# The products with v and with kv in two column halves of the TensorE array

## The chip, the cores and the metric

The kernel runs on one core of a Trainium2 chip. The metric is the device time of one execution in microseconds (us), lower is better; each number of a comparison is the median of several executions. Engines are named as the profile names them: PE is TensorE's matmul, PEld its weight load, DVE is VectorE, ACT is ScalarE, POOL is GpSimd, SP issues the transfers.

## The reference

Three stages follow each other: an attention with random features, a layer of experts of which each token takes one, and a gated feed-forward layer. The change lies in the first alone, so the other two are cut.

```python
# q, k, v: 4 batches, 8 heads, 576 tokens, 64 numbers; omega: 128 features x 64
def phi(x):
    proj = np.einsum('bhsd,md->bhsm', x, omega)
    h = proj - np.sum(x * x, axis=-1, keepdims=True) / 2.0
    h = h - np.max(h, axis=-1, keepdims=True)
    return np.exp(h) / np.sqrt(m)
q_p, k_p = (phi(q * scale), phi(k * scale))
kv = np.einsum('bhsm,bhsd->bhmd', k_p, v)
z = np.sum(k_p, axis=2)
num = np.einsum('bhsm,bhmd->bhsd', q_p, kv)
den = np.einsum('bhsm,bhm->bhs', q_p, z)[..., None] + 1e-06
attn = num / den
...  # then the experts (2304 tokens, 512 wide, 8 experts) and the gated layer
```

## The kernel before, in words

The 2304 tokens (4 batches of 576) are 18 tiles of 128 tokens. Since 576 is four tiles and a half, the fifth of each nine tiles holds 64 tokens of one batch and 64 of the next; the code calls its index within the nine `MID`. The attention goes in two groups of two batches, each with nine k tiles and then nine q tiles, so 36 units, one per step of the loop `for s in range(N + 3)` (L577). Inside `tc.manual_schedule()` (L566) the order in which the code writes the instructions is the order in which each engine gets them. One step works on several units at different depths.

A step of a k tile: `project` (L403, matmul at L409) multiplies the tile with omega, two heads at a time, one in rows 0 to 63 and one in rows 64 to 127 of the array; DVE reduces to row maxima (`maxima`, L419) and ACT takes the exponentials (`exps`, L435) into `ph`, 128 tokens by 8 heads by 128 features. One step later `kv_sum` calls `kv_part` (L440, matmul at L448): for each head the stationary operand is `ph` of that head (128 tokens by 128 features) and the moving operand is 96 columns of v (64 of this head, a one for the sum z, and 31 that nobody reads). The results add up over the tiles of a batch in PSUM. For the `MID` tile `kv_part` runs twice, with 64 rows each time.

A step of a q tile: after `project`, `maxima` and `exps` as above, `turn` (L478, L482) transposes `ph` on TensorE, `turned` (L484, L496) copies the result to SBUF as `qt` (half by DVE, half by ACT), `numerators` (L499, L505) multiplies `qt` of each head (128 features by 128 tokens, stationary) with 96 columns of the batch's kv, `divide` (L511) is DVE's, and `turn_x` (L531, L534) transposes the quotient on TensorE. On TensorE a step therefore reads `project` of unit s, `turn_x` of s-3, `numerators` of s-2 and `turn` of s-1, with the router's products (L218, L230) between some. For the `MID` tile the transposed features are copied into two buffers, `qa` and `qb`, whose other 64 columns POOL set to zero early on (L627, L628), and each head takes two products, one with the first batch's kv and one with the second's, that add up in PSUM.

The operands here are float32. In the trace such a matmul is two load-and-product pairs (16 pairs for eight heads); a transpose is one.

Of the kernel before, what the change touches and what calls it, by code (L numbers as in the profile page):

```python
# [10 lines left out]
F32 = mybir.dt.float32  # L11
# [16 lines left out]
def attention_moe_ffn_kernel(  # L28
# [4 lines left out]
    nc = tc.nc  # L33
    NTI, _, DM2 = qx.shape
    DM = DM2 // 2
    D, M = om.shape[0] // 2, om.shape[1] // 2
    H = DM // D
    VW = D + 1
# [8 lines left out]
    PT = NTI // NP  # L47
    MID = PT // 2
# [14 lines left out]
    def bank(*shape):  # L63
        return psum.tile([128, *shape], F32, tag="one", name="one")
# [4 lines left out]
    def third():  # L69
        return psum.tile([128, 2, 512], F32, tag="third", name="third", bufs=1)  # L70
# [41 lines left out]
    wk = p1.enter_context(tc.tile_pool(name="wk", bufs=2))  # L112
# [245 lines left out]
    units = [(kind, g * PT + i) for g in range(NP) for kind in "kq" for i in range(PT)]  # L358
# [5 lines left out]

    with p1:
        HALF = (slice(0, DM // 2), slice(DM // 2, DM))
        loads, st, kv, acc = {}, [{} for _ in units], {}, {}

        def load(s):
            kind, i = units[s]  # L370
            t = ld.tile([128, 2, DM], F32, tag="kq", name=f"{kind}{i}", bufs=4)
            src = (kx if kind == "k" else qx)[i].rearrange("p (a d) -> p a d", a=2)
            if s == 0:
                for part in ((0, HALF[0]), (0, HALF[1]), (1, slice(None))):
                    nc.sync.dma_start(out=t[:, part[0], part[1]], in_=src[:, part[0], part[1]])
            else:
                nc.sync.dma_start(out=t, in_=src)
            loads[s] = t

        def load_v(s):  # L380
            i = tile_of(s, "k")
            if i is not None:
                t = loads["v", i] = ld.tile([128, VR], F32, tag="v", name=f"v{i}", bufs=4)
                nc.sync.dma_start(out=t, in_=vx[i])

        def squares(s):
            xn = loads[s][:, 1].rearrange("p (h d) -> p h d", d=D)
            sq = wk.tile([128, H, D], F32, tag="sq", name="sq", bufs=3)
            nc.gpsimd.tensor_tensor(out=sq, in0=xn, in1=xn, op=ALU.mult)
            kind, i = units[s]  # L390
            w = D
            while w > (D // 4 if kind == "q" and i % PT > 1 else D):
                w //= 2
                nc.gpsimd.tensor_tensor(
                    out=sq[:, :, 0:w], in0=sq[:, :, 0:w], in1=sq[:, :, w:2 * w], op=ALU.add
                )
            st[s]["sq"] = sq[:, :, 0:w]
# [42 lines left out]
        def kv_part(s, bt, rows, first, last):  # L440
            ph, vt = st[s]["ph"], loads["v", units[s][1]]
            if first and bt % 2:
                a = third()
                acc[bt] = [a[:, j, 0:384] for j in range(2)]
            elif first:
                acc[bt] = [bank(384) for j in range(2)]
            for h in range(H):
                nc.tensor.matmul(  # L448
                    acc[bt][h // 4][:, h % 4 * 96:(h % 4 + 1) * 96],
                    ph[rows, h, :], vt[rows, h * VW:h * VW + 96],  # L450
                    start=(first and h % 4 == 0), stop=last, skip_group_check=True,
                )

        def kv_sum(s):
            g, i = divmod(units[s][1], PT)
# [26 lines left out]
                nc.tensor.transpose(st[s]["t"][h // 4][:, h % 4, :], ph[:, h, :], ident)  # L482

        def turned(s):  # L484

            g, i = divmod(units[s][1], PT)
            if i == MID:
                parts = [(qa, 2 * g, slice(0, 64)), (qb, 2 * g + 1, slice(64, 128))]
            else:
                qt = wk.tile([128, H, 128], F32, tag="qt", name="qt")  # L490
                parts = [(qt, 2 * g + int(i > MID), slice(0, 128))]
            for hf in range(2):
                for qt, _, cols in parts:
                    src = st[s]["t"][hf][:, :, cols]
                    dst = qt[:, 4 * hf:4 * hf + 4, cols]
                    (nc.scalar.copy if hf else nc.vector.tensor_copy)(dst, src)  # L496
            st[s]["q"] = parts

        def numerators(s):  # L499
            a = third()  # L500
            st[s]["a"] = a[:, :, 0:384].rearrange("p a (h w) -> p a h w", w=96)
            parts = st[s]["q"]
            for h in range(H):
                for n, (qt, bt, _) in enumerate(parts):
                    nc.tensor.matmul(  # L505
                        st[s]["a"][:, h // 4, h % 4, :], qt[:, h, :], kv[bt][:, h * VW:h * VW + 96],
                        start=(n == 0 and h % 4 == 0), stop=(n == len(parts) - 1),
                        skip_group_check=True,
                    )

        def divide(s):  # L511
# [41 lines left out]
        load(3)  # L553
        load_v(2)
        om_s = wk.tile([128, 2 * M], F32, name="om_s", bufs=1)
        qa = wk.tile([128, H, 128], F32, name="qa", bufs=1)
        qb = wk.tile([128, H, 128], F32, name="qb", bufs=1)

        route = [Routing(0)]
        first = None  # L560
# [5 lines left out]
        with tc.manual_schedule():  # L566
            p = third()
            for _ in range(13):
                nc.tensor.matmul(p[:, 0, 0:128], ones, ones, start=True, stop=True)
            nc.vector.tensor_scalar(  # L570
                out=om_s, in0=om_raw, scalar1=SCALE, scalar2=None, op0=ALU.mult
            )
            squares(0)
            squares(1)
            router = router_stationary(emb_t)
            rest = route[0].rest()
            for s in range(N + 3):  # L577
                clock[0] = s
                if s + 4 < N:
                    load(s + 4)  # L580
                load_v(s + 3)
                if tile_of(s - 2, "k") is not None:
                    kv_out(s - 2)
                if tile_of(s - 2, "q") is not None:
                    turned(s - 2)
                if s + 2 < N:
                    squares(s + 2)
                old = tile_of(s - 3, "q")
                if old is not None:
                    token_norms(s - 3)  # L590
                if s < N:
                    project(s)
                t = tile_of(s - 6, "q")
                if t is not None and t % 3 == 2:
                    route[-1].logits(t % PT // 3)
                base = s - (2 * PT + 2)
                if base >= 1:
                    next(rest, None)
                if base == PT + 4:
                    route.append(Routing(1))  # L600
                if old is not None:
                    turn_x(s - 3)
                t = tile_of(s - 4, "q")
                group = t is not None and t % 3 == 2
                if group:
                    route[-1].products(t % PT // 3)
                if s > 1:
                    next(router, None)
                if s < N:
                    norms(s)  # L610
                    maxima(s)
                    exps(s)
                if old is not None:
                    turned_x(s - 3)
                if group:
                    route[-1].products_out()
                if s == PT + 4:
                    next(router, None)
                if tile_of(s - 2, "q") is not None:
                    numerators(s - 2)  # L620
                    divide(s - 2)
                if tile_of(s - 1, "k") is not None:
                    kv_sum(s - 1)
                if tile_of(s - 1, "q") is not None:
                    turn(s - 1)
                if s == 2:
                    nc.gpsimd.memset(qa[:, :, 64:], 0.0)  # L627
                    nc.gpsimd.memset(qb[:, :, 0:64], 0.0)  # L628
                if s == N:
                    first = Expert(0)  # L630
                if N <= s < N + 2:
                    first.fetch(nc.gpsimd)
# [14 lines left out]
    with ExitStack() as p2:  # L647
# [111 lines left out]
        last = xs[LAST]  # L759
# [3 lines left out]
        with tc.If(totals[0] > 0):  # L763
            for bt in range(B):
                with tc.For_i(0, E) as e:
                    n = nc.values_load(
                        ext_i[0:1, bass.ds(e + bt * E, 1)], min_val=0, max_val=S,
                        skip_runtime_bounds_check_because=why,
                    )
# [64 lines left out]
    with ExitStack() as p3:  # L834
# [25 lines left out]
        for grp in range(NF // GF):  # L860
            wos, h2s = [], [[] for _ in blocks]
            for ff in range(GF):
                f = grp * GF + ff
                w = wgv.pop(f) if f in wgv else gate_val(f)
                for nb, (t0, n) in enumerate(blocks):
                    cols = slice(t0 * 128, (t0 + n) * 128)
                    ps = pair()[:, :, 0:n * 128]
                    for m in range(2):
                        k = 0
                        for c in range(NC):  # L870
                            for a, x in HALVES:
                                nc.tensor.matmul(  # L872
                                    ps[:, m], w[:, a, m, c, :], xp[:, c, x, cols],
                                    start=(k == 0), stop=(k == 3 * NC - 1),
                                )
                                k += 1
                    s = sp.tile([128, 512], F32, tag="s", name="s")[:, 0:n * 128]
                    nc.scalar.activation(out=s, in_=ps[:, 0], func=AF.Silu)  # L878
                    nc.vector.tensor_tensor(out=s, in0=ps[:, 1], in1=s, op=ALU.mult)  # L879
                    h = h2p.tile([128, 2, 512], F32R, tag="h2", name="h2")[:, :, 0:n * 128]  # L880
# [78 lines left out]
```

## Time and profile before

| | us |
|---|---|
| time, median of 3 runs | 833.69 (833.52 to 835.24) |
| time of the profiled execution | 835.67 |
| its span, first to last instruction | 833.9 |
| PE busy in the span | 815.9 (98%) |
| weight loads (PEld) busy | 731.2 (88%) |
| DVE, ACT, POOL busy | 534.2, 273.5, 166.6 |

Read it with care: matmuls are pipelined and the record of one is far longer than the time until the next can start, so a busy share of 98% does not say that the array is used to the full. The distance between the starts of two loads, one after the other, is the better measure. The attention takes the first 175 us or so; the rest of the span is the experts and the gated layer, which the change does not touch.

### The profile page before, as it was taken

Reading aid. Unit: us, or ns where it says so; the run is one execution under the profiler, and the core shown is the slowest. Engines: PE = TensorE matmul, PEld = TensorE weight load, DVE = VectorE, ACT = ScalarE, POOL = GpSimd, SP = SyncE. Lnnn points to the kernel's source line nnn. Section 1 sums busy time; section 2 is a strip of 40 time slices with the busy share of each in tenths; the row PEclk is TensorE's granted clock in tenths of the full one; section 3 lists DMA queues with packets and bytes.
Section 4 is the critical chain, followed back from the end, with each engine's and each line's share of the span. In section 5 each row is a group of like instructions: output and inputs, shape, how many; then the busy total and the mean of one; then the engine's idle time right before and its main releaser. Section 6 shows DMA issues by size and latency. Waiting matters only on the chain.

```text
span 833.9 us, 12850 instructions
## 1 busy us (share of the span) xinstructions
PE 815.9 (98%) x5158; PEld 731.2 (88%) x5159; DVE 534.2 (64%) x919; ACT 273.5 (33%) x630; POOL 166.6 (20%) x165
## 2 busy tenths in 40 slices
PE   8989998999999998999999999999999999999998
PEld 7979997899999998999888888888888888888886
DVE  3797788776342342489994039837963993697354
ACT  3577657743131322432323332212211221122120
POOL 4352144030000000802222111211111121112120
PEclk8999999999999999999999999999999999999999
DMA  7644563132322222332211002200210120020014
GB/s 254 199 133 134 152 193 104 51 96 99 91 81 98 90 76 44 127 101 76 77 51 50 1 1 76 76 1 26 76 51 0 54 74 26 25 77 26 1 49 178
DMA packets 23676, 66.64 MB, mean 80 GB/s; under 512 B 3104, under 2 KB 5680, under 8 KB 23608
## 3 DMA queue, kind: packets, MB, share of 16 engines
q1 hardware_dynamic: 23608, 65.74, 24.9%
q8 instruction: 42, 0.69, 0.3%
q14 instruction: 26, 0.21, 0.1%
HBM read 60.94 MB, written 4.79 MB: 79 GB/s over the span
## 4 chain that ended last, share of the span: by engine, by line
PE 60%; DVE 0%; issue 0%
PE two L872 24%; PE one L845 18%; PE third L872 12%; PE two L678 3%; PE third L698 2%; PE two L698 2%; PE third L678 1%; DVE y_acc L854 0%
## 5 line engine op out<-in xcount | busy, mean ns | idle before, releaser
L872 PE MATMUL two<-xp,wp 128*128 128x512 f32 (+1 forms) x960 | 209.5, 368 | 0.0
L872 PEld LDWEIGHTS two<-xp,wp 128*128 128x128 f32 x960 | 168.2, 188 | 31.4 <-DVE s L879 0.6
L845 PE MATMUL one<-wo,h 128*128 128x512 f32 x648 | 159.8, 390 | 0.0
L90 POOL TENSOR_TENSOR h<-s,h 128x512 fp32r<-128x512 f32 (+1 forms) x60 | 78.1, 1303 | 337.8 <-ACT h L89 337.8
L845 PEld LDWEIGHTS one<-wo,h 128*128 128x128 f32 x648 | 120.6, 188 | 24.8 <-DVE y_acc L854 0.3
L854 DVE TENSOR_TENSOR y_acc<-y_acc,one 128x512 f32<-128x512 f32 x90 | 61.5, 684 | 77.3 <-PE one L845 77.2
L872 PE MATMUL third<-xp,wp 128*128 128x512 f32 (+1 forms) x480 | 106.5, 368 | 0.0
L872 PEld LDWEIGHTS third<-xp,wp 128*128 128x128 f32 x480 | 84.4, 188 | 15.4
L435 ACT ACTIVATE ph<-two,bias 128x128 f32<-128x128 f32 x288 | 78.1, 384 | 39.5 <-DVE bias L426 28.9
L678 PE MATMUL two<-xp,wp 128*128 128x288 f32 x576 | 82.4, 302 | 3.8 <-DVEq L763 3.8
L678 PEld LDWEIGHTS two<-xp,wp 128*128 128x128 f32 x576 | 79.9, 194 | 4.1 <-ACT xp L89 4.0
L89 ACT CAST h<-s 128x512 fp32r<-128x512 f32 (+1 forms) x60 | 34.7, 579 | 77.6 <-DVE s L879 77.6
L89 ACT CAST wp<-raw 128x1024 fp32r<-128x1024 f32 x32 | 33.6, 1049 | 62.1 <-PE two L698 35.1
L879 DVE TENSOR_TENSOR s<-two,s 128x512 f32<-128x512 f32 (+1 forms) x40 | 25.3, 632 | 44.6 <-ACT s L878 44.4
L698 PE MATMUL third<-h,wp 128*128 128x288 f32 x384 | 52.5, 296 | 0.0
L698 PE MATMUL two<-h,wp 128*128 128x288 f32 x384 | 51.8, 296 | 0.0
L698 PEld LDWEIGHTS third<-h,wp 128*128 128x128 f32 x384 | 51.6, 189 | 0.0
L698 PEld LDWEIGHTS two<-h,wp 128*128 128x128 f32 x384 | 51.4, 189 | 0.0
L878 ACT ACTIVATE s<-two 128x512 f32<-128x512 f32 (+1 forms) x40 | 22.1, 553 | 89.3 <-PE two L872 89.3
L419 DVE TENSOR_REDUCE mx<-two 128x8 f32<-128x1024 f32 x36 | 43.8, 1217 | 9.8 <-PE two L409 9.4
L90 DVE TENSOR_TENSOR wp<-raw,wp 128x1024 fp32r<-128x1024 f32 x30 | 40.0, 1333 | 15.4 <-ACT wp L89 15.4
L90 POOL TENSOR_TENSOR xp<-y_f,xp 128x576 fp32r<-128x576 f32 x12 | 18.6, 1592 | 151.4 <-ACT xp L89 151.4
(160 smaller groups left out, 980.3 us busy)
## 6 DMA issues: line engine op xcount, KB each, us to landing
raw<-in_w_dram SPq DMA_DIRECT2D x68, 512.0 KB, 3.5
q<-in_qx_dram SPq DMA_DIRECT2D x18, 512.0 KB, 3.6
k<-in_kx_dram SPq DMA_DIRECT2D x17, 512.0 KB, 4.2
v<-in_vx_dram SPq DMA_DIRECT2D x18, 276.0 KB, 4.0
out_dram<-y_acc SPq DMA_DIRECT2D x18, 256.0 KB, 2.0
gate<-gts SPq DMA_DIRECT2D x4, 256.0 KB, 5.4
k<-in_kx_dram SPq DMA_DIRECT2D x2, 128.0 KB, 2.3
k<-in_kx_dram SPq DMA_DIRECT2D x1, 256.0 KB
```

What stands on the lines that cost most here:

```text
L89: nc.scalar.copy(hi, src)
L90: lo_eng.tensor_tensor(out=lo, in0=src, in1=hi.bitcast(F32), op=ALU.subtract)
L419: nc.vector.tensor_reduce(out=mx.rearrange("p (c a) -> p a c", a=2), in_=p.rearrange("p a (h m) -> p a h m", m=M), axis=AX.X, op=ALU.max,)
L435: nc.scalar.activation(out=ph[:, h, :], in_=p[:, h % 2, h // 2 * M:(h // 2 + 1) * M], func=AF.Exp, bias=bias[:, h:h + 1],)
L678: nc.tensor.matmul(ps[:, j], w[:, a, c, f * 128:(f + 1) * 128], xp[:, c, b, c0 + j * HB:c0 + (j + 1) * HB], start=(c == 0 and n == 0), sto ...
L698: nc.tensor.matmul(ps[:, j], w[:, a, f, :], h[:, b, j * HB:(j + 1) * HB], start=(f == 0 and n == 0), stop=(f == len(hs) - 1 and n == 2),)
L845: nc.tensor.matmul(p, h[:, x, i * 128:(i + 1) * 128], w[:, a, :], start=(k == 0), stop=(k == 3 * GF - 1),)
L854: nc.vector.tensor_tensor(out=dst, in0=dst, in1=p, op=ALU.add)
L872: nc.tensor.matmul(ps[:, m], w[:, a, m, c, :], xp[:, c, x, cols], start=(k == 0), stop=(k == 3 * NC - 1),)
L878: nc.scalar.activation(out=s, in_=ps[:, 0], func=AF.Silu)
L879: nc.vector.tensor_tensor(out=s, in0=ps[:, 1], in1=s, op=ALU.mult)
```

## The change

`kv_part` and `numerators` give each head two matmuls in place of one: one with the first 64 columns of the stationary operand, whose result goes to PSUM partitions 0 to 63, and one with the other 64 columns, whose result goes to partitions 64 to 127. The moving operand of both is the same 96 columns, but for the `MID` tile of q, where the first half takes the kv of the first batch and the second half that of the next. That tile so needs one `qt` like all others: `qa`, `qb`, their copies and the two memsets go.

```diff
+        COLS = (slice(0, 64), slice(64, 128))
...
             for h in range(H):
-                nc.tensor.matmul(
-                    acc[bt][h // 4][:, h % 4 * 96:(h % 4 + 1) * 96],
-                    ph[rows, h, :], vt[rows, h * VW:h * VW + 96],
-                    start=(first and h % 4 == 0), stop=last, skip_group_check=True,
-                )
+                for f in COLS:
+                    nc.tensor.matmul(
+                        acc[bt][h // 4][f, h % 4 * 96:(h % 4 + 1) * 96],
+                        ph[rows, h, f], vt[rows, h * VW:h * VW + 96],
+                        start=(first and h % 4 == 0), stop=last, skip_group_check=True,
+                    )
...
         def turned(s):
-            g, i = divmod(units[s][1], PT)
-            if i == MID:
-                parts = [(qa, 2 * g, slice(0, 64)), (qb, 2 * g + 1, slice(64, 128))]
-            else:
-                qt = wk.tile([128, H, 128], F32, tag="qt", name="qt")
-                parts = [(qt, 2 * g + int(i > MID), slice(0, 128))]
+            qt = st[s]["q"] = wk.tile([128, H, 128], F32, tag="qt", name="qt")
             for hf in range(2):
-                for qt, _, cols in parts:
-                    src = st[s]["t"][hf][:, :, cols]
-                    dst = qt[:, 4 * hf:4 * hf + 4, cols]
-                    (nc.scalar.copy if hf else nc.vector.tensor_copy)(dst, src)
-            st[s]["q"] = parts
+                (nc.scalar.copy if hf else nc.vector.tensor_copy)(
+                    qt[:, 4 * hf:4 * hf + 4, :], st[s]["t"][hf]
+                )
...
             for h in range(H):
-                for n, (qt, bt, _) in enumerate(parts):
+                for n, t in enumerate(COLS):
+                    bt = 2 * g + int(2 * i + n > 2 * MID)
                     nc.tensor.matmul(
-                        st[s]["a"][:, h // 4, h % 4, :], qt[:, h, :], kv[bt][:, h * VW:h * VW + 96],
-                        start=(n == 0 and h % 4 == 0), stop=(n == len(parts) - 1),
-                        skip_group_check=True,
+                        st[s]["a"][t, h // 4, h % 4, :], qt[:, h, t],
+                        kv[bt][:, h * VW:h * VW + 96],
+                        start=(h % 4 == 0), stop=True, skip_group_check=True,
                     )
...
-        qa = wk.tile([128, H, 128], F32, name="qa", bufs=1)
-        qb = wk.tile([128, H, 128], F32, name="qb", bufs=1)
...
-                if s == 2:
-                    nc.gpsimd.memset(qa[:, :, 64:], 0.0)
-                    nc.gpsimd.memset(qb[:, :, 0:64], 0.0)
```

On TensorE one step of a q tile (the sixth) stands thus before; a row is a line of the code, the output and the inputs, the size of the output and the number of matmuls (`third` is the PSUM of the numerators, `one` that of the transposes, `two` that of `project`):

```order
L409 MATMUL two_823<-om_s_127,q5_568 128x128 x8
L534 MATMUL one_832<-ident_74,x_797 128x128 x4
L505 MATMUL third_855<-kv0_409,qt_814 128x96 x8
L482 MATMUL one_869<-ident_74,ph_777 128x128 x4
L482 MATMUL one_870<-ident_74,ph_777 128x128 x4
L409 MATMUL two_893<-om_s_127,q6_613 128x128 x8
```

And the same place of the change:

```order
L411 MATMUL two_923<-om_s_127,q5_644 128x128 x8
L532 MATMUL one_932<-ident_74,x_897 128x128 x4
L503 MATMUL third_955<-kv0_453,qt_914 64x96 x16
L485 MATMUL one_977<-ident_74,ph_869 128x128 x4
L485 MATMUL one_978<-ident_74,ph_869 128x128 x4
L411 MATMUL two_1000<-om_s_127,q6_689 128x128 x8
```

No row has moved; the eight products between the two transposes have become sixteen that write 64 partitions each. So it is in each k tile with L448, which has L409 (rows in halves) ahead of it and behind it.

For the `MID` tile of q the first products of two heads stand thus on TensorE before (16 such rows in all):

```order
L218 MATMUL one_908<-xp_97,en_st_104 128x384 x8
L505 MATMUL third_936<-kv0_409,qa_128 128x96
L505 MATMUL third_936<-kv1_570,qb_129 128x96
L505 MATMUL third_936<-kv0_409,qa_128 128x96
L505 MATMUL third_936<-kv1_570,qb_129 128x96
```

And in the change (16 rows too):

```order
L218 MATMUL one_1015<-xp_97,en_st_104 128x384 x8
L503 MATMUL third_1043<-kv0_453,qt_991 64x96
L503 MATMUL third_1043<-kv1_646,qt_991 64x96
L503 MATMUL third_1043<-kv0_453,qt_991 64x96
L503 MATMUL third_1043<-kv1_646,qt_991 64x96
```

Their number and order stay; each now has 64 stationary columns, as in all other tiles. At the seam from the attention to the experts the scheduler sets two of DVE's and one of ACT's instructions of the first expert products (L684, L685) one to five places later than before.

## Rows read from the trace of the kernel before

**Rows 1.** Busy time by stretch: length, busy us of each engine, granted clock, DMA share, GB/s.

```profile
13.30:23.50 10.20, 10.20 (x61) 9.41 (x60) 4.23 (x13) 4.72 (x19) 5.04 (x6) 0.50 0.65 216
23.50:44.80 21.30, 20.93 (x218) 19.60 (x217) 17.72 (x38) 13.19 (x49) 8.30 (x11) 1.00 0.66 198
44.80:92.60 47.80, 46.02 (x448) 42.12 (x448) 41.12 (x87) 36.10 (x117) 16.79 (x21) 1.00 0.42 131
92.60:124.20 31.60, 30.79 (x311) 28.81 (x309) 25.32 (x66) 18.85 (x69) 10.33 (x13) 1.00 0.61 185
124.20:175.80 51.60, 48.03 (x444) 43.98 (x443) 39.44 (x97) 36.24 (x111) 13.90 (x17) 1.00 0.24 76
```

**Rows 2.** The weight loads in order of time, one q step: start us, us, count.

```profile
62.66 0.97 PEld L409 LDWEIGHTS two<-om_s,q 64*128 64x128 f32 x16 [0.17 <-issue]
63.75 0.42 PEld L534 LDWEIGHTS one<-ident,x 128*128 128x128 f32 x4
64.14 1.86 PEld L505 LDWEIGHTS third<-kv,qt 128*128 128x128 f32 x16
65.90 0.99 PEld L482 LDWEIGHTS one<-ident,ph 128*128 128x128 f32 x8
67.06 0.97 PEld L409 LDWEIGHTS two<-om_s,q 64*128 64x128 f32 x16 [0.17 <-issue]
```

**Rows 3.** Weight loads by line and shape, first 176 us: busy us, mean ns.

```profile
L505 PEld LDWEIGHTS third<-kv,qt 128*128 128x128 f32 x256 | 30.1, 192 | 3.5 <-ACT qt L496 2.2 <-issue 1.2
L409 PEld LDWEIGHTS two<-om_s,q 64*128 64x128 f32 x288 | 17.5, 187 | 2.6 <-issue 2.0
L482 PEld LDWEIGHTS one<-ident,ph 128*128 128x128 f32 x144 | 16.4, 143 | 2.8 <-DVE xp L541 1.4
```

**Rows 4.** Weight loads in order of time: transposes that move 8 and 128 columns.

```profile
59.35 0.32 PEld L188 LDWEIGHTS one<-ident,es 8*128 8x128 f32 x4 [0.17 <-issue]
...
73.56 0.91 PEld L482 LDWEIGHTS one<-ident,ph 128*128 128x128 f32 x8
```

**Rows 5.** Weight loads in order of time, MID tile of q: first and last of 16 rows.

```profile
69.95 0.36 PEld L505 LDWEIGHTS third<-kv,qa 128*128 128x128 f32 x2
...
73.36 0.30 PEld L505 LDWEIGHTS third<-kv,qb 128*128 128x128 f32 x2
```

**Rows 6.** Busy time by stretch (columns of rows 1): one q step, and the MID step.

```profile
62.66:67.06 4.40, 4.40 (x45) 4.00 (x44) 4.06 (x10) 3.42 (x12) 2.23 (x3) 1.00 0.40 119
67.06:74.63 7.57, 7.53 (x69) 7.20 (x68) 4.52 (x12) 4.77 (x17) 1.04 (x1) 1.00 0.32 109
```

**Rows 7.** DVE in order of time: waits for `project` in a q and a k step.

```profile
63.87 1.22 DVE L419 TENSOR_REDUCE mx<-two 128x8 f32<-128x1024 f32 x1 [0.20 <-PE two L409]
...
104.32 1.22 DVE L419 TENSOR_REDUCE mx<-two 128x8 f32<-128x1024 f32 x1 [0.99 <-PE two L409]
```

**Rows 8.** Weight loads in order of time, products with v, five of the k tiles.

```profile
15.78 3.48 PEld L448 LDWEIGHTS one<-v,ph 128*128 128x128 f32 x16 [0.22 <-ACT e L178]
...
21.45 2.83 PEld L448 LDWEIGHTS one<-v,ph 128*128 128x128 f32 x16 [0.22 <-issue]
...
25.47 1.86 PEld L448 LDWEIGHTS one<-v,ph 128*128 128x128 f32 x16
...
111.82 1.86 PEld L448 LDWEIGHTS third<-v,ph 128*128 128x128 f32 x16
...
118.24 2.10 PEld L448 LDWEIGHTS third<-v,ph 128*128 128x128 f32 x16 [0.31 <-ACT ph L435]
```

**Rows 9.** PE in order of time, MID tile of k: products in different row halves.

```profile
107.53 1.69 PE L448 MATMUL one<-v,ph 64*128 64x96 f32 x13
108.95 0.35 PE L448 MATMUL third<-v,ph 64*128 64x96 f32 x1
109.06 0.27 PE L448 MATMUL one<-v,ph 64*128 64x96 f32 x1
```

**Rows 10.** All that touches qa: count, duration ns min/median/max, first and last start.

```profile
L496 DVE COPY qa<-one x2: 412/414/415, 67.4 to 148.0; 128x256 f32<-128x256 f32 x2
L496 ACT COPY qa<-one x2: 424/426/427, 67.9 to 148.5; 128x256 f32<-128x256 f32 x2
L627 POOL MEMSET qa<- x1: 524/524/524, 16.6 to 16.6; 128x512 f32 x1
```

More of the change, by code (lines that the diff above doesn't have):

```diff
@@ L501, in numerators @@
             st[s]["a"] = a[:, :, 0:384].rearrange("p a (h w) -> p a h w", w=96)
-            parts = st[s]["q"]
+            qt = st[s]["q"]
+            g, i = divmod(units[s][1], PT)
             for h in range(H):
-                for n, (qt, bt, _) in enumerate(parts):
+                for n, t in enumerate(COLS):
+                    bt = 2 * g + int(2 * i + n > 2 * MID)
                     nc.tensor.matmul(
-                        st[s]["a"][:, h // 4, h % 4, :], qt[:, h, :], kv[bt][:, h * VW:h * VW + 96],
-                        start=(n == 0 and h % 4 == 0), stop=(n == len(parts) - 1),
-                        skip_group_check=True,
+                        st[s]["a"][t, h // 4, h % 4, :], qt[:, h, t],
+                        kv[bt][:, h * VW:h * VW + 96],
+                        start=(h % 4 == 0), stop=True, skip_group_check=True,
                     )
```

## The prediction

> **What bounds the kernel now.** I first cut the span into stretches [rows 1]. Up to 175.8 us is the attention, the only part that the change touches. TensorE has something in hand in nearly all of it (46.0 of 47.8 us in the first q stretch, 30.8 of 31.6 in the second k stretch), but a busy record says little of a pipelined engine, so I went on to the order of the weight loads. One q step [rows 2] takes 4.40 us from one `project` (L409) to the next, and in it the groups of loads follow each other with at most 0.17 us between them: TensorE is full. DVE is nearly as full, 4.06 of the 4.40 us [rows 6], and its one wait there is 0.20 us, for `project` [rows 7]. So in q steps TensorE sets the pace and DVE stands some 0.3 us behind it. In k steps it is mixed. At 104.32 DVE waits 0.99 us for `project` [rows 7], so TensorE leads there; at 118.24 the load group of the product with v is stretched to 2.10 us and waited 0.31 us for ACT's exponentials, where the dense form, at 25.47 and 111.82, takes 1.86 [rows 8]. From the list of all k tiles I count eight dense groups at the full clock, two at the half clock (15.78 and 21.45, where the granted clock is 0.50, so 1.2 GHz [rows 1]), four stretched by ACT, the first tile, whose exponentials are just being made, and the `MID` tile that is split by rows, twice.
>
> **The price of one pair.** What limits a product with 128 stationary and 96 moving columns? The 16 loads of L505 take 1.86 us, the last one's record being 0.192: (1.86 - 0.192)/15 = 0.111 us from one to the next [rows 2, 3]. A transpose that moves 128 columns comes each (0.91 - 0.143)/7 = 0.110 us [rows 3, 4], one that moves 8 columns and also loads 128 each 0.32/4 = 0.080 at most [rows 4], so the 0.110 is the moving: 0.86 ns for a column. If float32 products move at that rate, 96 columns take 0.082 us, less than 0.111, so L505 and L448 are bound by loading: 0.87 ns a column, 0.056 us for 64.
>
> With two column halves a head's pass needs two loads of 64 columns and two moves of 96. No row of the trace has a product on half of the columns. The nearest has half of the rows: `project` runs two heads in two row halves, and its 16 loads take (0.97 - 0.187)/15 = 0.052 us each, so 0.104 for a pair with 128 moving columns [rows 2, 3]. There both halves move side by side, which one after the other would need 2 x 0.110. In the `MID` tile of k the first product for `third` even starts (108.95) ahead of later ones for `one` [rows 9], though all of `one` stand ahead in the order. Carried over to column halves, a pair costs what one half's moves cost, 0.082 us instead of 0.111 to 0.112. The bounds: 0.056 if products move faster than transposes do and the load of one half decides; 0.112 if the two loads must take turns (2 x 0.056); 0.164 if the moves must (2 x 0.082). I take 0.082, since the row halves are the nearest row by far.
>
> The Trainium skill (TensorE: Matmul & The Clock Gate, part 3, measured speedup) gives 2.38 times for three column tiles with 512 moving columns, so moves side by side; no run here shows it yet. The same part of the Trainium skill says that a load overlaps products in flight only when its row group differs, which here would forbid overlap altogether; the trace disagrees already, since the loads of L505, all on the same 128 rows, follow at 0.111 us, which leaves no room for a move of 0.082 in between.
>
> **The price of changing the array's shape.** In the q step `project` ends its loads at 63.63 and the transposes begin at 63.75, 0.12 later; from `turn` (66.89) to `project` it is 0.17. Between full-size groups the next begins before the record of the last has ended: -0.03 from `turn_x` to L505, -0.10 from L505 to `turn` [rows 2]. So entering or leaving another shape costs about 0.145 + 0.065 = 0.21 us. In a q tile the products now differ in shape from the transposes ahead of them and behind them [rows 2]: two new changes, 0.42 us. In a k tile `project` stands on both sides and differs already: nothing new.
>
> **The sum.**
> 1. The two `MID` tiles of q. Before, 32 loads from 69.95 to 73.66, (3.71 - 0.19)/31 = 0.1135 us each [rows 5], 3.63 us together, and the step takes 7.57 us against 4.40 [rows 6]. After, 16 pairs of 0.082 = 1.31, plus 0.42. That is -1.90 us each, -3.8 together. DVE, busy 4.52 us in that step [rows 6], does not stop it at 5.7 us.
> 2. The other q tiles: 16 x (0.112 - 0.082) = 0.48 us gained, 0.42 lost, so -0.06. I count 14 of 16, since the first of each stretch waits for copies anyway (2.2 us for ACT's in all [rows 3]): -0.8 us.
> 3. The k tiles: eight dense groups gain 0.48 us each, 3.8. At the half clock a pair costs twice: the full group at 15.78 (3.48 us) gains 16 x (0.21 - 0.164) = 0.7, the one at 21.45, part of it at the full clock, some 0.6. Together 5.1 us. But DVE is busy 25.3 of 31.6 us there [rows 1] and ACT waits for it, so the lead passes to them soon. I take half, -2.6, with 0 and -5.1 as bounds. The stretched groups gain nothing, and the `MID` tile about nothing: its pairs get cheaper but its shape no longer is that of `project` next to it.
> 4. The copies of the `MID` tile: two of 0.41 us on DVE become one of the size that other tiles copy, and likewise on ACT (0.42 each) [rows 10]. TensorE sets that step, so 0; without that cover at most the 0.41 of one copy a tile. The two memsets on POOL (0.52 each at 16.6 us [rows 10]) lie in a stretch in which POOL is busy 5.0 of 10.2 us [rows 1]: 0, at most 1.0. The instructions that the scheduler shifted at the seam to the experts have matmuls to hide behind; 0.
>
> Sum: -3.8 - 0.8 - 2.6 = -7.2 us. The profiled execution took 835.67 us, span 833.9 and 1.8 around it, so it would take 828.5. It stood 2.0 above the median of the runs, 833.69; taking the difference over to the median gives **826.5 us**. With pairs between 0.075 and 0.090 us and the share of item 3 between none and all, this case's own range is 822 to 831.
>
> **The rivals.**
> *Loads take turns* (chance 0.20), the one on the other side. If the array can be loaded for only one column half at a time, a pair costs 0.112, as before. The k tiles gain nothing, the two `MID` tiles still 3.63 - 1.79 - 0.42 = 1.42 each, -2.8, and 14 q tiles pay the 0.42 for nothing: +5.9. Sum +3.1: 836.8 us. For it: loading bounds these products already, and half the columns do not make two halves fewer. Against it: the row halves load side by side. Items 1 to 3 together change by 0.34 us for each ns of the pair's price, so the point from which this rival decides is a pair of 0.103 us.
> *A cheaper pair or no pause* (0.15). At 0.056 us a pair, q tiles would gain 0.48 net but DVE allows only some 0.3, 14 x 0.3 = 4.2; `MID` 2 x (3.63 - 0.90 - 0.42) = 4.6; k tiles half of (8 x 0.9 + 2.2) = 4.7. Sum -13.5: 820.2 us. Pairs at 0.082 but no pause at the change of shape: 4.2 + 4.6 + 2.6 = 11.4, 822.3 us. For it: nothing shows that moving a float32 product is as slow as a transpose. Against the second: `project` shows the pauses.
> *Moves take turns* (0.08). A pair at 0.164 us: 14 q tiles at +0.83 + 0.42 give +17.5, the `MID` tiles -1.2, the dense k groups 8 x 0.83 = 6.7 and those at the half clock about 3. Sum +26: 860 us.
> *Loads hide behind nothing* (0.02). If no load may run beside a move, each half costs its load and its move, 0.138, a pair 0.276: 30 tiles (14 of q, 16 of k) at 16 x 0.164 = +2.6 and the pauses, about +86, so 920 us. The 0.111 of L505 [rows 2, 3] speaks against it. This is what the sentence on row groups in the Trainium skill (TensorE: Matmul & The Clock Gate, part 3) would give, read strictly.
> *The clock falls* (0.03). If the smaller products let the granted clock fall in the q or k stretches as it does from 13.3 to 23.5 us [rows 1], each such 10.2 us costs about 5 us, and it would eat most of the gain.
>
> **How the numbers follow.** The forecast's case has 0.52. About 0.2% (1.7 us) is what a measurement of this kernel can tell from no change, so "same" is 832.0 to 835.4. Faster: 0.48 of the forecast's case and the cheaper one, 0.63. Same: 0.08, the forecast's upper end and the lower end of the first rival. Slower: 0.29, the first rival's rest, the three after it. The range 820 to 838 holds nearly all of the forecast, most of the cheaper case and most of the first rival, about 0.8.
>
> **What the profile after would show.** Two loads of L503 or L451 starting within a few ns, pairs 0.08 us apart, a load group of x32 in about 1.4 us: the price of the pair. If they stand singly 0.056 apart, 1.8 us a group, the first rival. About 0.3 us from `turn_x`'s last load to L503's first, and again to `turn`: the pauses. The `MID` step at about 5.7 us in place of 7.57, other q steps within 0.2 us of 4.3. DVE's waits for `project` in k steps shorter than 0.99 us, and ACT or DVE named more often in TensorE's waits. Wrong above all would make it a pair price over 0.103 us, or pauses far from 0.21 us.

## The result and the profile after

The changed kernel takes **824.15 us** (median of 4 runs, 823.77 to 825.67) beside 833.61 us of the kernel before, measured with it (4 runs, 832.90 to 835.24): a ratio of 0.9887 [0.9868, 0.9906], 9.5 us less. The forecast was 826.5 us. The profiled execution took 824.23 us, its span is 822.5 us.

First the weight loads in order of time, in the `MID` step of q (62.58 to 68.17) and the plain step after it (L411, L503, L485 and L532 were L409, L505, L482 and L534). They answer to [rows 2] and [rows 5].

```profile
62.58 0.97 PEld L411 LDWEIGHTS two<-om_s,q 64*128 64x128 f32 x16 [0.17 <-issue]
63.67 0.42 PEld L532 LDWEIGHTS one<-ident,x 128*128 128x128 f32 x4
64.07 1.35 PEld L218 LDWEIGHTS one<-xp,en_st 128*128 128x128 f32 x8
65.67 1.35 PEld L503 LDWEIGHTS third<-kv,qt 128*64 128x64 f32 x32 [0.25 <-issue]
67.14 0.85 PEld L485 LDWEIGHTS one<-ident,ph 128*128 128x128 f32 x8
68.17 0.97 PEld L411 LDWEIGHTS two<-om_s,q 64*128 64x128 f32 x16 [0.17 <-issue]
69.26 0.42 PEld L532 LDWEIGHTS one<-ident,x 128*128 128x128 f32 x4
69.84 1.35 PEld L503 LDWEIGHTS third<-kv,qt 128*64 128x64 f32 x32 [0.17 <-issue]
71.32 0.86 PEld L485 LDWEIGHTS one<-ident,ph 128*128 128x128 f32 x8
```

The 32 loads of one `numerators` take 1.35 us; one load's record is 0.136 (its mean in the next view), so the 16 pairs follow at (1.35 - 0.14)/15 = 0.081 us, and the trace has the two loads of a pair 7 ns apart. The pauses are there too: L503 begins 0.16 us after the last record of L532 ends (69.26 + 0.42 to 69.84), `turn` 0.13 after L503 (69.84 + 1.35 to 71.32), where [rows 2] had -0.03 and -0.10.

The same loads grouped by line, first 168 us, answering to [rows 3]:

```profile
L503 PEld LDWEIGHTS third<-kv,qt 128*64 128x64 f32 x576 | 24.5, 136 | 7.2 <-issue 4.5 <-ACT qt L490 2.7
```

Now the stretches. The first begins with the span, the others at the first `project` load of units 10, 19 and 28, and the last ends at the experts' first product, so before and after hold the same work. Columns are those of [rows 1]; last come the plain q step, the `MID` step and the plain step behind it. Before:

```profile
0.00:44.76 44.76, 40.72 (x347) 38.30 (x348) 27.80 (x63) 21.56 (x77) 17.49 (x36) 0.89 0.69 222
44.76:89.34 44.58, 42.80 (x413) 39.02 (x412) 37.95 (x82) 34.16 (x112) 15.76 (x20) 1.00 0.43 136
89.34:124.18 34.84, 34.03 (x343) 31.93 (x343) 28.52 (x72) 20.79 (x73) 11.37 (x14) 1.00 0.58 174
124.18:169.29 45.11, 41.54 (x391) 37.59 (x391) 36.56 (x92) 32.98 (x105) 13.06 (x17) 1.00 0.24 75
```

After:

```profile
0.00:40.33 40.33, 35.35 (x507) 30.47 (x508) 28.00 (x63) 21.51 (x77) 16.64 (x35) 0.96 0.77 251
40.33:82.59 42.26, 39.67 (x525) 33.54 (x523) 37.32 (x80) 34.10 (x111) 15.73 (x20) 1.00 0.46 140
82.59:115.32 32.73, 31.76 (x519) 27.05 (x519) 28.12 (x72) 20.78 (x73) 11.36 (x14) 1.00 0.63 187
115.32:157.93 42.61, 38.79 (x503) 32.23 (x502) 36.74 (x93) 32.80 (x104) 12.98 (x18) 1.00 0.25 79
58.33:62.58 4.25, 4.25 (x62) 3.59 (x61) 3.75 (x10) 3.42 (x12) 2.24 (x3) 1.00 0.44 120
62.58:68.17 5.59, 5.59 (x70) 4.93 (x69) 4.61 (x11) 4.70 (x16) 1.04 (x1) 1.00 0.45 152
68.17:72.34 4.17, 4.17 (x61) 3.60 (x60) 3.86 (x10) 3.09 (x10) 1.04 (x1) 1.00 0.41 138
```

The three stretches at the full clock give 2.32, 2.11 and 2.50 us, 6.93 together. The first gives 4.43, and there the mean granted clock differs as well, 0.89 and 0.96. That sum, 11.36 us, is the whole difference of the two profiled executions (835.67 - 824.23 = 11.44): the experts give and take nothing. The `MID` step fell from 7.57 us [rows 6] to 5.59.

DVE's waits up to the end of the second k stretch are the other half of [rows 7] (what waited, for whom: us in total, times, longest). Before, to 125 us:

```profile
DVE mx L419 <- PE two L409: 9.4, 8, 3.1
```

After, also to 125 us:

```profile
DVE mx L421 <- PE two L411: 5.0, 8, 2.6
```

Nearly all of that difference lies in the first stretch, in which the clock differs too (8.2 us before, 3.9 after). In the second k stretch one such wait is left in each, 1.0 and 0.4 us.

### The profile page after: what moved, and what is told of

It reads as the page before. It is cut to its first block, busy times and chain, and to the rows that moved or that the text cites. A ratio compares the mean times of both kernels' runs of the same rounds, so it can differ in the third digit from the quotient of the medians.

```text
span 822.5 us, 13988 instructions
## 1 busy us (share of the span) xinstructions
PE 802.4 (98%) x5734; PEld 707.4 (86%) x5735; DVE 533.1 (65%) x917; ACT 273.1 (33%) x628; POOL 165.8 (20%) x163
## 4 chain that ended last, share of the span: by engine, by line
PE 60%; DVE 0%; issue 0%
PE two L865 24%; PE one L838 18%; PE third L865 12%; PE two L671 3%; PE third L691 2%; PE two L691 2%; PE third L671 1%; DVE y_acc L847 0%
```

## The experiments

Two theories stood against each other. **S**: the gain is the sum of the prediction, spread over the `MID`, the other q and the k tiles. **C**: what goes beyond the sum is TensorE's granted clock, which spends less time at 0.50 (1.2 GHz) near the start. The kernels were measured in three series, each beside the kernel before. The runs of one kernel spread over some 6 us and follow their mean clock: a straight line through the 71 runs of the first series, with a level for each kernel, falls by 0.33 us for each us less at half the clock. "At equal clock" below is the difference of two such levels, with its 95% interval; the later series have slopes of 0.37 (without `before_w66`) and 0.41.

**The change again, and its parts.** `after_again` is the changed kernel once more.

> The change once more, unaltered, for a second profile and a tighter time. Two theories on where more than the forecast 7.2 us came from. Theory S (the sum): pairs at 0.082 us, pauses of about 0.2 us, and the k tiles keeping more of their gain than the half that I gave them. Theory C (the clock): the stretch at the half clock near the start, 10.2 us long in the profile of before and 3.4 us in the profile of the change, is worth some 3 us, and it is shorter because the early products with v are. Both expect a time of 9 to 10 us under before. C expects the short stretch (3.4 us) again in this profile; if its length is chance, it may be 10.2 us here.

`kv_only`: the kernel before with the product with v in column halves and nothing else.

```diff
-                nc.tensor.matmul(acc[bt][h // 4][:, h % 4 * 96:(h % 4 + 1) * 96],
-                    ph[rows, h, :], ...
+                for f in COLS:
+                    nc.tensor.matmul(acc[bt][h // 4][f, h % 4 * 96:(h % 4 + 1) * 96],
+                        ph[rows, h, f], ...
```

> Only the products with v run in column halves; the numerators stay as before, with padded copies. My sum gives -2.6 us (0 to -5.1). Theory S expects -3 to -5, with the half-clock stretch as long as before, 10.2 us. Theory C expects -4 to -6 with the stretch at 3.4 us, most of the gain before 45 us of the span.

`num_only`: the changed kernel with these lines taken back, so column halves in `numerators` alone.

> Only the numerators run in column halves (no padded copies); the products with v stay as before. My sum gives -3.8 for the two shared tiles and -0.8 for the others, -4.6 us. Both theories expect -4 to -6; C expects the half-clock stretch as long as before (10.2 us), since nothing ahead of 45 us has changed but two memsets.

`mid_only`: `num_only` with halves only in the `MID` tile; the other q tiles take 128 columns at once, without padded copies.

```diff
-                for n, t in enumerate(COLS):
+                for n, t in enumerate(COLS if i == MID else (slice(0, 128),)):
```

> Column halves in the numerators of the two shared tiles alone, all other products whole as before. My sum gives -3.8 us, 0.8 less than with all numerators in halves: each other q tile should gain 0.48 by its pairs and lose 0.42 by two changes of the array's shape. If the pauses cost less than I read, the version with all numerators in halves is ahead by more; if the pairs cost more, this one is ahead.

| kernel (before: 833.32, 29 runs) | median us | ratio | mean clock | at equal clock |
|---|---|---|---|---|
| before | 833.32 | 1 | 0.9918 | 0 |
| after_again | 824.01 | 0.9888 [0.9863, 0.9913] | 0.9940 | -8.3 ± 0.8 |
| kv_only | 830.57 | 0.9965 [0.9950, 0.9979] | 0.9926 | -2.8 ± 0.6 |
| num_only | 828.88 | 0.9949 [0.9932, 0.9965] | 0.9920 | -4.3 ± 0.6 |
| mid_only | 831.56 | 0.9979 [0.9960, 0.9998] | 0.9913 | -2.3 ± 0.6 |

The v part and the kv part add up: 2.8 + 4.3 = 7.1 us, near the sum of the forecast, and the whole is a little more. The gain of `kv_only` stays under what either theory expected, and the half clock followed neither: the profile of `kv_only` has none up to 165 us, and `num_only` and `mid_only`, with the old products with v, have 3.4 us near the start, as `after` and `after_again` have. `mid_only` came out smaller than the two `MID` steps of the trace (2 x 1.98), so it was run once more below.

**The clock at the start.** If C holds, work that keeps TensorE going early should take the clock's part from both kernels. Eleven products with `ones`, whose result nobody reads, go behind the second `project`:

```diff
+                if s == 1:
+                    p = third()
+                    for _ in range(11):
+                        nc.tensor.matmul(p[:, 0, 0:128], ones, ones, start=True, stop=True)
```

> The kernel before, with eleven extra matmuls on ones (their result is never read) put behind the second project, where TensorE otherwise has nothing for 3 us. Theory C (the length of the half-clock stretch near the start is worth about 0.4 us for each of its us, and it comes and goes with the idle time there) expects no half-clock stretch before 45 us and a time 1 to 4 us under before. If the stretch does not depend on that idle time, it stays and the time is that of before.

> The change with the same eleven extra matmuls. Theory C expects no half-clock stretch before 45 us and a time 0.5 to 2 us under the change. What the change is worth at an equal clock is this time less that of before_warm: the sum of the prediction says -7.2 us; with the k tiles keeping more than half of their gain it is -8 to -9.

`before_warm` took 830.10 us (7 runs, 0.9965 [0.9941, 0.9989]), `after_warm` 822.60 (5 runs, 0.9866 [0.9845, 0.9888]), beside 833.70: the change is worth 7.5 us between them. Here are their stretches, cut like those above but for the second border, which is unit 18. `before_warm`, and last the piece of it at half the clock:

```profile
0.00:39.70 39.70, 38.28 (x368) 36.14 (x369) 28.24 (x63) 21.61 (x77) 16.09 (x35) 1.00 0.75 245
39.70:80.74 41.04, 39.11 (x360) 35.30 (x360) 33.25 (x72) 29.63 (x97) 16.10 (x21) 0.96 0.41 131
80.74:121.14 40.40, 39.71 (x395) 37.36 (x395) 33.34 (x82) 25.55 (x89) 12.43 (x15) 1.00 0.58 171
121.14:166.35 45.21, 41.58 (x391) 37.58 (x391) 36.77 (x92) 33.04 (x105) 13.06 (x17) 1.00 0.23 76
46.80:50.20 3.40, 3.21 (x15) 3.21 (x16) 1.43 (x5) 2.32 (x9) 0.78 (x2) 0.50 0.07 29
```

`after_warm`:

```profile
0.00:39.33 39.33, 37.36 (x528) 32.46 (x529) 28.19 (x63) 21.95 (x79) 14.80 (x32) 1.00 0.74 251
39.33:75.47 36.14, 33.68 (x457) 28.55 (x455) 32.13 (x70) 29.11 (x96) 16.43 (x21) 1.00 0.45 147
75.47:113.62 38.15, 37.20 (x587) 31.94 (x586) 32.91 (x82) 25.55 (x89) 12.32 (x15) 1.00 0.59 183
113.62:156.23 42.61, 38.86 (x504) 32.24 (x503) 36.71 (x93) 32.87 (x104) 13.04 (x18) 1.00 0.23 79
```

With the clock at 1.00 in both, the first stretch differs by 0.37 us in place of 4.43. But a stretch from 0.00 also holds the time until the first `project`, which differs from one execution to the next (6.45 and 6.94 us in these two). So here is the way from the first load of `project` to that of unit 10, in `before`, `num_only`, `mid_only`, `after`, `after_again`, `before_warm`, `after_warm` and `kv_only`, in this order:

```profile
6.73:44.76 38.03, 35.08 (x322) 32.77 (x321) 26.90 (x59) 21.54 (x76) 15.46 (x20) 0.87 0.69 225
6.51:41.71 35.20, 32.44 (x321) 30.06 (x320) 27.88 (x59) 21.54 (x76) 13.98 (x17) 0.95 0.74 240
6.58:41.73 35.15, 32.38 (x322) 30.23 (x321) 28.18 (x59) 21.60 (x77) 14.59 (x18) 0.95 0.72 241
6.30:40.33 34.03, 30.14 (x482) 25.37 (x481) 27.09 (x59) 21.50 (x76) 14.72 (x19) 0.95 0.79 258
6.28:40.81 34.53, 30.14 (x481) 25.35 (x480) 28.13 (x59) 21.50 (x76) 14.03 (x17) 0.95 0.75 253
6.45:39.70 33.25, 32.92 (x343) 30.89 (x342) 27.10 (x59) 21.59 (x76) 14.03 (x18) 1.00 0.76 250
6.94:39.33 32.39, 31.52 (x503) 26.82 (x502) 26.80 (x59) 21.93 (x78) 12.73 (x15) 1.00 0.75 262
6.85:39.24 32.39, 28.20 (x481) 23.97 (x480) 26.98 (x59) 21.54 (x76) 14.94 (x19) 1.00 0.77 267
```

`num_only` and `mid_only` have the products with v of the kernel before and the 3.4 us of half clock of the change. So the shorter half clock is worth some 2.9 us (38.03 to 35.20 and 35.15), and the halves of the products with v are worth 0.6 to 1.2 us at that clock (to 34.53 and 34.03) and 0.86 at the full clock (33.25 to 32.39). Of the 11.4 us between the two profiled executions 2.9 was then the clock (10.2 us of half clock before, from 13.3 to 23.5, 3.4 after, from 12.4 to 15.8) and 0.4 the earlier first `project`. These are single executions: `after` and `after_again`, the same kernel, are 0.5 apart.

C holds for the size of that, not for its reason: the piece is as short in `num_only` and `mid_only`, whose early products are the old ones. What C expected of the eleven products came: in both warm profiles there is no half clock before 45 us, and both times lie in its ranges. `before_warm` is 3.6 us faster than the kernel before, at equal clock 0.8 ± 0.9, so most of that is clock (the mean of its runs is 0.9951, that of the kernel before 0.9920). `after_warm` shows no half clock in the attention at all, `before_warm` 3.4 us at 46.8.

**The columns moved.** If a pair of halves costs what one half's moves cost, fewer moved columns make it cheaper, and do nothing for the full-width form, which is bound by loading. Of the 96 columns that are moved for a head, 65 are read later (`VW`); these kernels move 66, in both products (the outputs are cut to 66 likewise).

```diff
-                        ph[rows, h, f], vt[rows, h * VW:h * VW + 96],
+                        ph[rows, h, f], vt[rows, h * VW:h * VW + 66],
...
-                        kv[bt][:, h * VW:h * VW + 96],
+                        kv[bt][:, h * VW:h * VW + 66],
```

> The change with 66 moving columns in place of 96. If moving bounds the column halves at 0.86 ns a column, the pair falls from 0.082 to 0.057 us, and a q tile's sixteen pairs by 0.4 us; DVE allows about 0.2 of it in plain q tiles, 0.4 in those with the router's products: together with half of the gain in k tiles 4 to 8 us under the change. If a floor other than moving holds the pair at 0.082, no change.

> The kernel before, with 66 moving columns in place of 96 in the products with v and with kv (the columns left out are read by nobody). If loading 128 columns bounds these products, as the prediction has it, the pitch of the loads stays at 0.111 us and the time is that of before within 0.3%. If moving bounds them, the pitch falls towards 0.08 and the time by 10 us or more.

`after_w66` took 821.43 us (5 runs, 0.9844 [0.9824, 0.9864]). In its `MID` tile and the next, the weight loads in order of time:

```profile
66.16 1.02 PEld L503 LDWEIGHTS third<-kv,qt 128*64 128x64 f32 x32 [0.25 <-issue]
...
69.95 1.02 PEld L503 LDWEIGHTS third<-kv,qt 128*64 128x64 f32 x32 [0.17 <-issue]
71.04 0.42 PEld L485 LDWEIGHTS one<-ident,ph 128*128 128x128 f32 x4
71.77 0.42 PEld L485 LDWEIGHTS one<-ident,ph 128*128 128x128 f32 x4 [0.30 <-DVE xp L539]
```

A pair now takes (1.02 - 0.14)/15 = 0.059 us; 0.082 x 66/96 = 0.056 was to come if moving sets it. So with 96 columns moving sets it. With 66 the load of a half, 0.056 us by the prediction's price, is as long as the move, and this run can't tell the two. Of the 0.33 us by which the group got shorter, the plain step behind `MID` keeps 0.09 (4.17 to 4.08), because `turn` now waits 0.30 us for DVE, and the one ahead of it 0.01 (4.25 to 4.24). The first `MID` step, where DVE has room, keeps all of it (5.59 to 5.21), the second 0.21 (5.59 to 5.38). The time is 2.7 us under that of the change, less than the 4 to 8 expected; at equal clock it is -12.3 ± 0.8 beside -8.3 ± 1.0 for `after_warm`, 4.0 less.

`before_w66` took 857.41 us (6 runs, 1.0265 [1.0224, 1.0306]), 24 more where no change was expected. A row of its loads, and its windows:

```profile
81.81 1.86 PEld L505 LDWEIGHTS third<-kv,qt 128*128 128x128 f32 x16
```

```profile
12.30:66.90 54.60, 54.60 (x319) 51.49 (x320) 24.71 (x59) 22.80 (x86) 16.58 (x22) 0.50 0.43 137
66.90:128.40 61.50, 60.79 (x602) 56.55 (x602) 49.56 (x114) 42.28 (x140) 18.33 (x22) 1.00 0.47 150
128.40:155.70 27.30, 27.30 (x161) 25.36 (x161) 15.21 (x41) 12.87 (x49) 8.77 (x12) 0.50 0.34 108
```

At the full clock the group is the 1.86 us of [rows 2], so moving does not bound the full-width form, and loading is what is left, as the forecast had it. But for 54.6 and 27.3 us the granted clock was 0.50, though TensorE had something in hand all the time. By the mean clock of the runs, 0.957 beside 0.992, there are some 59 us more of half clock, so the 24 us are about 0.40 for each, near the slopes above.

**The `MID` tile again, and an order that might remove DVE's wait.** `mid_only_warm` is `mid_only` with the eleven early products. `after_w66_warm` is `after_w66` with them. The two swap kernels move `numerators` of tile s - 2 from ahead of `divide` to right behind `project`, ahead of `turn_x`, once with 96 columns and once with 66.

```diff
                 project(s)
+                if tile_of(s - 2, "q") is not None:
+                    numerators(s - 2)
...
-                    numerators(s - 2)
                     divide(s - 2)
```

> Column halves in the numerators of the two shared tiles alone, with the eleven extra matmuls that keep the clock up near the start. The sum gives -3.8 us against before_warm; the earlier time without the extra matmuls came out at -1.8 to -2.3 while its trace shows 1.98 us less in each of the two steps, which theory C would put down to half-clock stretches that fall elsewhere in its runs. C expects -3.5 to -4.3 here at like clocks; if it is again -2, the two steps give something back later.

> The change with the extra matmuls and with the numerators written ahead of the transposes of x, so that a plain q step has three changes of the array's shape in place of four. By the price of the pause (0.2 us) up to 16 x 0.2 = 3.2 us less than after_warm; DVE and the copies of qt, which are wanted earlier, leave 1 to 2.5. If the pauses hide behind waits anyway, no change.

> The change with 66 moving columns and the extra matmuls. Both gains are in different places, so 2.0 to 3.0 us less than after_warm (822.6), near 820 us.

> 66 moving columns, numerators ahead of the transposes of x, and the extra matmuls. With the pair at 0.057 us plain q steps wait for DVE already, so the swap should give under 1 us over after_w66_warm, or cost something where the numerators wait for their copies.

| kernel (before: 834.63, 26 runs) | median us | ratio | at equal clock |
|---|---|---|---|
| mid_only_warm | 829.85 | 0.9957 [0.9926, 0.9987] | -3.7 ± 1.0 |
| after_swap_warm | 834.03 | 1.0007 [0.9987, 1.0027] | +1.4 ± 1.0 |
| after_w66_warm | 820.49 | 0.9836 [0.9806, 0.9865] | -12.9 ± 1.3 |
| swap_w66_warm | 826.32 | 0.9906 [0.9877, 0.9935] | -6.3 ± 1.1 |

`mid_only_warm` now agrees with the trace's 3.96 us, though some of its gain may be that of the eleven products (0.8 ± 0.9 at equal clock, in the second series). The runs of this kernel span 825.5 to 837.2 us, at mean clocks of 0.998 to 0.984: a median alone says little here.

The swap costs about 10 us (+1.4 at equal clock, where `after_warm` stands at -8.3 in its own series) in place of the 1 to 2.5 us that it was to bring. TensorE's waits tell why; in `after_warm`, 40 to 158 us:

```profile
PE one L485 <- DVE xp L539: 1.3, 2, 0.8
```

In `after_swap_warm`, 45 to 170 us:

```profile
PE one L485 <- DVE xp L539: 11.7, 10, 1.6
```

And one step of `after_swap_warm` in order of time:

```profile
61.55 0.66 PE L532 MATMUL one<-ident,x 128*128 128x128 f32 x4
...
62.24 0.59 ACT L535 CAST xp<-one 128x512 fp32r<-128x512 f32 x1 [1.79 <-PE one L532]
...
62.86 0.69 DVE L539 TENSOR_TENSOR xp<-one,xp 128x512 fp32r<-128x512 f32 x1 [0.87 <-ACT xp L535]
...
63.60 0.66 PE L485 MATMUL one<-ident,ph 128*128 128x128 f32 x4 [0.97 <-DVE xp L539]
```

`turn_x` now comes after `numerators`; ACT waits 1.79 us for it, DVE 0.87 for ACT, and the second half of `turn` 0.97 for the bank that DVE still reads. `numerators` was the work behind which that chain was hidden.

The fastest version run is `after_w66_warm` at 820.49 us, with `after_w66` (821.43) beside it and not told apart; at equal clock the 66 columns save some 4 us more than the change itself.

## Why the prediction was right

The direction, the mechanism and the time (2.3 us off, inside the case's own range) hold. What the sum left out is the clock. Point by point, from the profiled pair:

- **The pair's price**, taken as 0.082 us from the row halves: 0.081, two loads 7 ns apart. The rivals at 0.112, 0.164 and 0.276 fall by this row, and `after_w66` and `before_w66` show that moving limits the halves with 96 columns and does not limit the full width. The row-group sentence of the Trainium skill (TensorE: Matmul & The Clock Gate, part 3), which the case of 920 us came from, does not describe these loads: the pairs, all on the same 128 rows, come every 0.081 us, which leaves no time for a load apart from the moves. The prediction read the row halves of `project` at 0.104 us a pair, as 15 equal distances. Their two loads also start 7 ns apart, so 16 loads have 7 distances, and a pair takes (0.97 - 0.187)/7 = 0.112 us, about the 0.110 of 128 moved columns. The rule that a pair costs the moves of one half fits better than the prediction knew.
- **The pauses**, 0.42 us a q tile: 0.16 + 0.03 and 0.13 + 0.10, 0.42.
- **`MID` tiles**, -1.90 each: 7.57 to 5.59, -1.98, in both q stretches; `mid_only_warm` bears it out in time, `mid_only` only half of it (2.3 ± 0.6 at equal clock), and why is open.
- **Other q tiles**, -0.8 together: the two q stretches give 2.32 + 2.50, less 2 x 1.98, so 0.86. That this meets the sum is in part luck: it had 0.06 for each of 14 tiles, but the steps beside `MID` gain 0.14 and 0.15 (4.31 to 4.17, 4.40 to 4.25), the next one nothing (4.67 and 4.66). In the step of 0.15 the group of L505 became 0.51 us shorter, not 0.48, and `turn` 0.06.
- **k tiles**, -2.6, half of what the groups could give: 2.11 in the second k stretch, which also holds one tile's numerators, and 0.86 in the first at the full clock (`before_warm` to `after_warm`), 3.0; `kv_only` at equal clock 2.8. In the second the lead passes as forecast: a group that was dense before (111.82, 1.86 us) is stretched after (102.83, 1.90 us), and DVE's one wait for `project` fell from 1.0 to 0.4 us. The prediction counts 17 of the 18 k tiles; the one that it leaves out (114.87, 2.00 us) is a fifth stretched group, which gains nothing in the sum.
- **Copies, memsets, seam**, 0: nothing in the stretches is left for them to explain; no run has them alone.

These make 3.96 + 0.86 + 2.11 + 0.86 = 7.8 us against 7.2 forecast; the warm medians differ by 7.5, and at equal clock the change is worth 8.3 ± 0.8. The term that was missing is the clock. It was a rival with the opposite sign, three chances in a hundred that smaller products let it fall. In the first series the mean clock rose from 0.9918 to 0.9940, which at the slope above is 1.2 us (0.0022 of 830 us, twice that in us at half clock, 3.7, times 0.33); the four runs behind the 824.15 stand at 0.9928, which would be 0.5. So 8.3 to 9.0 of the 9.5 us are accounted for, and the rest is inside the interval of the ratio, 7.8 to 11.0 us. Why the clock stays up longer with the change stays open, and whether it always does: the mean of `after_w66` is 0.9924, hardly above that of the kernel before, 0.9920.

## What to carry to other kernels

These float32 products with 128 columns loaded came every 0.111 us, whether 96 or 66 columns moved. In two column halves of the array loads and moves ran side by side, and a pair cost 0.081 us with 96 columns moved and 0.059 with 66. Each border to products of another shape cost about 0.2 us, so halves pay where a tile has many such products in a row or where they replace padded duplicates. Before a shorter group is booked as gain, look in the same step for the engine that is next: here DVE stood 0.3 us behind, and a cut of 0.33 us a tile left 0.09 of it in one plain step and 0.01 in another. Where runs differ in mean clock, compare at equal clock or in stretches at one clock, begun at the same instruction and not at the span's start, or some us of clock or of start are taken for the change.

## What was not expected of the hardware

- In `before_w66` moving 66 columns in place of 96, at the same pitch of loads, took the granted clock to 0.50 for 54.6 and 27.3 us, in which TensorE had no idle time in the profile; all six runs took 852.05 to 861.60 us. `after_w66` moves as few columns and shows 3.4 us. No run tells what makes the difference.
- The early piece at half clock lasted 10.2 us in the kernel before, 3.4 in the changed one, and `kv_only` had none up to 165 us (mean granted clock 1.00). In all six profiles with the eleven products that early piece is missing. In five of them there is another, later in the attention (3.4 us at 46.8 in `before_warm`, 10.2 at 103.3 and 3.4 at 127.1 in `mid_only_warm`), in `after_warm` there is none.
